# Moving the last token tile's products, its Gelu and four loads at the end of layer one's token loop

## The chip, the core and the metric

The kernel runs on one core of a Trainium2 chip. The metric is the device time of one launch in microseconds (us), the median of several runs. A core has five engines that run side by side and wait for each other by semaphores: TensorE (PE) multiplies matrices and writes the results to PSUM banks, VectorE (DVE) and ScalarE (ACT) do elementwise work and empty the banks, GpSimd (POOL) does elementwise work and issues some DMAs, and SyncE (SP) issues most DMAs. Each of them works through its own instructions strictly in the order in which the program issued them. So an instruction that waits holds up everything behind it on its engine.

## What is computed

Two layers, each a linear attention block and a gated block over 2048 tokens of width 512, all in float32. The change lies in the gated block of the first one:

```python
x = x + _A_ref(_layernorm(x), A_wqkv, A_wo)
x = x + _B_ref(_layernorm(x), B_w_in, B_w_sp, B_b_sp, B_w_out)     # and both once more: layer two

def _B_ref(x, w_in, w_sp, b_sp, w_out):
    z = _gelu(jnp.einsum("bsd,df->bsf", x, w_in))     # 512 -> 1792
    z1 = z[..., :896]
    z2 = _layernorm(z[..., 896:], axis=-1)
    g = jnp.einsum("ts,bsf->btf", w_sp, z2) + b_sp[None, :, None]
    return jnp.einsum("bsf,fd->bsd", z1 * g, w_out)
```

## The kernel before

Every float32 matrix product is made of three passes over operands that are split in two: a high part `h` (ScalarE copies the value into the rounded type, `high`, L220) and the rest `l` (VectorE subtracts, `low`, L223), and PE adds `h*h`, `h*l` and `l*h`. Big products are cut by a seven-product scheme (seven block products in place of eight), for which VectorE first forms sums and differences of blocks. They are called the fifth, sixth, seventh block and so on by the number of their product.

The program is unrolled; the order in which Python calls the helpers is the order on each engine. Three kinds of buffers matter here, each handed out by a first-in, first-out list: `pages` (22 tiles of 128x512), `quads` (6 tiles of 128x2048, which hold split weights and blocks) and `banks` (8 PSUM banks). A new owner of a buffer waits until the old owner's last reader is done. The sixth block's split takes the quad that held the high part of `xT[2]`, and P4's first raw weights the one that held its low part.

**The token loop.** `P2.run` takes the 16 token tiles of layer one (L = 0) through a pipeline of steps `s` = 1 to 18 (NT = 16). In a step, `c` finishes the attention of tile s-1, `d_high` and `d_low` transpose and split tile s-2 into `self.xT` (four tiles together make 512 tokens, so `xT[2]` are tiles 8 to 11 and `xT[3]` tiles 12 to 15), `e` multiplies tile s-3 with the second half of `w_in` into two banks, `e2` applies Gelu to them (L1076), `e3` takes the mean and variance (for tiles 14 and 15 on VectorE, `stats`, L365 and L367, with three small GpSimd instructions, L369 to L372), and `e4` normalises (L378). `first_a`, `first_b` and `first_out` (steps 15 to 17) begin the first half z1 for tokens 1024 to 2047. In steps 16 and 17 `e` and `e2` of tiles 13 and 14 stand near the head of the step; tile 15's stand after `tsplit(6)` and `e4(13)` in step 18.

**The blocks of `xT`.** z1 for the last 1024 tokens is made by the seven-product scheme: `raw(0)` and `raw(1)` (L1168) rebuild two blocks of `xT[2]` as h + l into the quad `self.B`; `T1` (L1202, L1203) turns the first into the fifth block, `T1split` splits it; `T2` makes two pairs of pages, `t2` (the sixth block, L1214 and L1216) and `b22` (the seventh, L1218 and L1219); `tsplit(6)` and `tsplit(7)` split these.

**The end.** `tail` then multiplies: `f(True)` for one piece of z1, three products with the fifth block `T[5]` into banks `v`, three with the sixth `T[6]`, three with the seventh `T[7]`, three with `xT[3]` itself, and three with `T[4]` (all `fmul`, L1161 to L1163, six matmuls each). Its results go through Gelu (`out`, L1151) and are stored to DRAM (L1153). The weights for `T[7]` come by six POOL DMAs (L211, `wfetch`) that are issued at the end of step 17.

**The spatial product.** `P4` follows: `w_sp` times z2, in steps `g`. Step g needs the raw weights (`fetch`, SP DMAs, L1743), their split (`sp`: `wsp`, L1764 on ScalarE and L1767 on VectorE) and the split part of z2 (`zahead`: L1872 and L1876, or L1852 to L1858 and then L220 and L223), then twelve matmuls (`mm`, L1989 to L1991). The raw weights live in halves of two quads, so the load of step g+4 waits until the split of step g has read its half. The four bias rows of `b_sp` are loaded by `loadb` (L2020, four SP DMAs into four pages): in layer one behind step g = 0 of P4, in layer two inside `tail`. They are first added at the end of P4's step 3.

Of the kernel before, what the change touches and what calls it, by code (L numbers as in the profile page):

```python
# [10 lines left out]
F32 = mybir.dt.float32  # L11
# [8 lines left out]
NT = S // P  # L20
# [138 lines left out]
def mixer_kernel(ctx: ExitStack, tc: tile.TileContext, x_in, wqkv, wo_d, win1_d, win2_d, wsp_d, bsp_d, wout_d,  # L159
# [671 lines left out]
    class P2:  # L831
# [378 lines left out]
        def T2(self):  # L1210
            h, l = (t.bitcast(F32) for t in self.xT[3])
            self.b22, self.t2 = ([pages.get(PAGE) for _ in range(2)] for _ in range(2))
            for c in range(2):
                nc.vector.tensor_add(self.b22[c], h[:, 2 + c], l[:, 2 + c])  # L1214
            for c in range(2):
                nc.vector.tensor_sub(self.t2[c], self.b22[c], self.B[:, 0, c])  # L1216
            for c in range(2):
                nc.vector.tensor_sub(self.b22[c], self.b22[c], h[:, c])  # L1218
                nc.vector.tensor_sub(self.b22[c], self.b22[c], l[:, c])  # L1219
# [11 lines left out]
        def tail(self):  # L1231
            V, A = nc.vector, nc.scalar.activation
            h, l = (t.bitcast(F32) for t in self.xT[3])
            L = self.L
# [48 lines left out]
            if L:  # L1283
# [2 lines left out]
                self.e4(NT - 4)  # L1286
                self.e4(NT - 3)
            quads.put(self.B)
            self.p4.fetch(3)
            ws = []  # L1290
            for f in range(3):
# [33 lines left out]
        def run(self, sums):  # L1325
# [4 lines left out]
            for s in range(1, NT + 3):  # L1330
# [42 lines left out]
                        self.d_high(s - 2)  # L1373
                        self.d_low(s - 2)
                if s == NT + 1:
                    self.raw(0)
                    self.T1()
                    self.T1split()
                    self.T2()
                    self.raw(1)  # L1380
                if s == NT + 2:
                    quads.put(*self.xT.pop(2))
                    self.tsplit(6)
                if s >= 4 and s != E4LATE:
                    self.e4(s - 4 - (s > E4LATE))
                self.qturn.load(s + 2)
                self.xturn.load(s - 1)
                if s >= 3:
                    if s not in (NT, NT + 1):
                        self.e(s - 3)  # L1390
                        self.e2(s - 3)
                    self.e3(s - 3)
                for _ in range(FONE.get(s, 0)):
                    self.f()
                if s in (15, 16, 17):
# [9 lines left out]
                    self.fsums.split(WADD[s - 1])  # L1405
                if s == NT:
                    self.B = quads.get([P, 2, 2, 512])
                    self.wf.extend(w1sums[f, 1] for f in range(3))
                self.fq.extend(self.fnext)
                self.fnext = []  # L1410
# [58 lines left out]
        def run2(self):  # L1469
            late = self.p1  # L1470
            for s in range(1, NT + 3):
# [5 lines left out]
                if s in self.qturn.by_pe:  # L1477
                    self.c(s - 1)
                    self.b_high(s)
                    self.c2(s - 1)  # L1480
                    late.late_phi_b()
                    self.b_low(s)
                    if s >= 2:
                        self.d_high(s - 2)
                        self.d_low(s - 2)
                    late.late()
                    self.c3(s - 1)
                    self.a2(s + 2)
                    late.late_phi_a()
                    self.a(s + 3)  # L1490
                else:
                    def b():
                        if s < NT:
                            self.b_high(s)

                    def bl():
                        if not pair:
                            self.a2_den(s + 2)
                        if s < NT:
                            self.b_low(s)  # L1500
                        if pair:
                            self.a2_den(s + 2)

                    if not pair:
                        if s >= FIRSTPAIR + 3:
                            self.a(s + 3)
                        b()
                        bl()
                    if s <= NT:
                        self.c(s - 1)  # L1510
                        self.c2(s - 1)
                    if s == NT:
                        quads.put(*self.W2)
                        pages.put(self.zbc)
                    ahead = s - 2 in self.xturn.by_pe

                    def turn():
                        self.d_high(s - 2)
                        self.d_low(s - 2)

                    def p():
                        self.a2_mul(s + 2)

                    def q():
                        if ahead:
                            turn()
                        if s <= NT:
                            self.c3(s - 1)
                        if pair or s < FIRSTPAIR + 3:
                            self.a(s + 3)  # L1530

                    def r():
                        if s <= NT + 1 and not ahead:
                            turn()

                    if pair:
                        def bp():
                            bl()
                            p()

                        def g():
                            if s - 6 >= FIRSTPAIR:
                                self.e4(s - 6)
                                self.e4(s - 5)

                        def ld():
                            self.wfetch()
                            self.wfetch()

                        if s == NT - 2:  # L1550
                            self.epair(s - 4, b, bp, q, r)
                        elif s == NT:
                            def q4():
                                q()
                                self.e4(NT - 8)
                                self.e4(NT - 7)

                            self.epair(s - 4, q4, ld, r)
                        elif s > NT:
                            def late4():  # L1560
                                self.T1split()
                                self.first_out(1, 2)
                                self.e4(NT - 6)
                                self.e4(NT - 5)

                            def late3():
                                self.raw(1)
                                quads.put(*self.xT.pop(2))
                                self.T2()
                                self.e3(NT - 4, False)  # L1570
                                self.e3(NT - 3, False)

                            self.epair(s - 4, late4, late3)
                        else:
                            self.epair(s - 4, b, bp, q, r, g)
                    elif s < FIRSTPAIR + 3:
                        p()
                        q()
                        r()
                    else:  # L1580
                        self.odd(s, p, q, r)
# [115 lines left out]
    class P4:  # L1697
# [622 lines left out]
        def run(self, nxt):  # L2320
            p2 = self.p2
            early = nxt is None
# [15 lines left out]
            for g in range(n):  # L2338
# [14 lines left out]
                    self.sums.tick()  # L2353
                if nxt is not None:
                    self.sums.halve(PARTS.get((p, k), -1), self.mark)
                if not early and g == 0:
                    self.loadb()
                if p in self.div:
                    if p == "P4" and k == 0 and "P5" in self.div:
                        for j in range(2):  # L2360
# [109 lines left out]
```

## Time and profile before

| | |
|---|---|
| median of 3 runs | 1349.79 us (1348.66 to 1350.32) |
| the profiled execution | 1349.34 us, of which 1347.6 us are the span of its instructions |
| PE | busy 1336.6 us, 99% of the span |
| DVE, ACT, POOL | busy 1074.6, 739.1 and 461.3 us |
| mean granted PE clock | 0.998 of full speed |
| layer one's token loop and tail | 129 to 352 us of the span: PE busy 218.4 of 223 us |
| layer one's P4 and after it | 352 to 683 us: PE busy 329.8 of 331 us |

A row of the timeline gives the start and the duration in us, the engine, the line, the operation, what it writes and reads, its shape, and how often it stands there in a row; in brackets stands how long the engine was idle before it and whom it waited for. Matmuls overlap: one of 128x512 lasts 0.39 us but the next starts 0.227 us after it. A row of the waits gives who waited for whom, the sum, how many times, and the longest.

### The profile page before, as it was taken

To read this page: it belongs to the slowest core of one execution; us is meant where nothing else is said; L and a number is where in the kernel's file an instruction comes from. 1 tells how busy PE (TensorE), PEld (TensorE's weight loads), DVE (VectorE), ACT (ScalarE), POOL (GpSimd) and SP (SyncE) were. 2 spreads that over 40 slices of the span, in tenths; PEclk is the share of its full clock that TensorE was granted. 3 is DMA by queue.
4 is the path that set the end of the run, shared out by engine and by line. 5 is a ranking of instruction groups with operands and counts; after the bars stand their busy time and mean duration, and the time that the engine had idled before them with its cause. 6 is when DMAs were issued, how large, how long until landed. Compare 5 with 4: busy or idle time off the path is not lost.

```text
span 1347.6 us, 19239 instructions
## 1 busy us (share of the span) xinstructions
PE 1336.6 (99%) x6533; PEld 1139.5 (85%) x6533; DVE 1074.6 (80%) x1687; ACT 739.1 (55%) x1250; POOL 461.3 (34%) x611
## 2 busy tenths in 40 slices
PE   9999999998999999999999999999999999999998
PEld 7888888887888888889988888888888888888898
DVE  7779877767799899898866778678689758899885
ACT  5764544445752256354666665557687433666454
POOL 3755775442026400301423444554531013122021
PEclk9999999999999999999999999999999999999999
DMA  5898599975879996794774562688777555579344
GB/s 183 292 307 271 169 299 293 302 225 196 266 252 377 332 295 191 271 319 94 178 159 129 132 154 73 193 240 262 236 220 234 167 161 174 176 243 319 123 76 66
DMA packets 172594, 291.34 MB, mean 216 GB/s; under 512 B 14544, under 2 KB 53456, under 8 KB 172240
## 3 DMA queue, kind: packets, MB, share of 16 engines
q1 hardware_dynamic: 153376, 250.92, 56.1%
q0 software_dynamic: 18976, 39.07, 13.6%
q8 instruction: 51, 0.84, 0.3%
q14 instruction: 47, 0.39, 0.1%
q10 hardware_dynamic: 144, 0.13, 0.0%
HBM read 205.39 MB, written 101.45 MB: 228 GB/s over the span
## 4 chain that ended last, share of the span: by engine, by line
PE 95%; DVE 2%; DMA 1%; ACT 1%; issue 0%; SPq 0%; POOL 0%; ACTq 0%; DVEq 0%
PE bank L234 13%; PE bank L236 13%; PE bank L235 13%; PE bank L1990 12%; PE bank L1991 12%; PE bank L1989 12%; PE bank L2187 3%; PE bank L2188 3%; PE bank L2189 3%; PE bank L1161 1%; PE bank L1163 1%; PE bank L1162 1%; PE bank L990 1%; PE bank L992 1%; PE bank L991 1%; PE bank L390 1%
## 5 line engine op out<-in xcount | busy, mean ns | idle before, releaser
L1989 PE MATMUL bank<-qd,pg 128*128 128x512 f32 x736 | 286.7, 390 | 0.7 <-ACT pg L1827 0.7
L1990 PE MATMUL bank<-qd,pg 128*128 128x512 f32 x736 | 286.6, 389 | 0.5 <-DVE qd L1767 0.5
L1991 PE MATMUL bank<-qd,pg 128*128 128x512 f32 x736 | 286.6, 389 | 0.0
L1764 ACT ACTIVATE qd<-qd 128x1024 fp32r<-128x1024 f32 x142 | 149.2, 1053 | 127.6 <-PE bank L1991 94.4
L1767 DVE TENSOR_TENSOR qd<-qd,qd 128x1024 fp32r<-128x1024 f32 x132 | 165.7, 1257 | 40.6 <-ACT qd L1764 40.4
L236 PE MATMUL bank<-qd,pg 128*128 128x512 f32 x448 | 174.8, 390 | 0.0
L1989 PEld LDWEIGHTS bank<-qd,pg 128*128 128x128 f32 x736 | 138.2, 188 | 30.0 <-ACT pg L1827 1.1
L1990 PEld LDWEIGHTS bank<-qd,pg 128*128 128x128 f32 x736 | 138.2, 188 | 29.5 <-DVE qd L1767 1.0
L1991 PEld LDWEIGHTS bank<-qd,pg 128*128 128x128 f32 x736 | 138.2, 188 | 28.9 <-DVE pg L1829 0.3
L2030 POOL TENSOR_TENSOR bg<-bg,pg 128x512 f32<-128x512 f32 x28 | 49.9, 1784 | 189.7 <-ACT qd L1764 92.9
L234 PE MATMUL bank<-qd,pg 128*128 128x512 f32 x264 | 103.3, 391 | 0.2 <-ACT pg L220 0.2
L235 PE MATMUL bank<-qd,pg 128*128 128x512 f32 x264 | 103.0, 390 | 0.0
L236 PEld LDWEIGHTS bank<-qd,pg 128*128 128x128 f32 x448 | 84.1, 188 | 18.1 <-DVE pg L223 0.4
L1673 POOL TENSOR_TENSOR pg<-pg,pg 128x512 f32<-128x512 f32 x48 | 70.0, 1458 | 71.8 <-DMA pg<-in_wsp_dram 64.5
L369 POOL TENSOR_SCALAR rs<-mv 128x1 f32<-128x1 f32 x76 | 23.8, 313 | 184.4 <-DVE mv L367 180.2
L2189 PE MATMUL bank<-wo,qd 128*128 128x256 f32 x288 | 81.5, 283 | 0.0
L2187 PE MATMUL bank<-wo,qd 128*128 128x256 f32 x276 | 78.2, 283 | 0.0
L2188 PE MATMUL bank<-wo,qd 128*128 128x256 f32 x276 | 78.1, 283 | 0.0
L220 ACT ACTIVATE pg<-pg 128x512 fp32r<-128x512 f32 (+1 forms) x86 | 49.9, 592 | 42.2 <-DVE pg L1858 20.0
L223 DVE TENSOR_TENSOR pg<-pg,pg 128x512 fp32r<-128x512 f32 (+1 forms) x84 | 54.7, 660 | 10.0 <-ACT pg L220 8.5
L549 POOL TENSOR_TENSOR pg<-pg,pg 128x512 f32<-128x512 f32 x30 | 39.9, 1331 | 59.8 <-DVE pg L543 58.0
L234 PE MATMUL bank<-bg,qd 128*128 128x448 f32 x160 | 59.0, 369 | 0.0
(297 smaller groups left out, 3361.8 us busy)
## 6 DMA issues: line engine op xcount, KB each, us to landing
qd<-s SPq DMA_DIRECT2D x62, 512.0 KB, 4.6
qd<-in_wsp_dram SPq DMA_DIRECT2D x40, 512.0 KB, 4.4
qd<-hP SPq DMA_DIRECT2D x40, 512.0 KB, 4.6
pg<-z SPq DMA_DIRECT2D x56, 256.0 KB, 5.3
pg<-in_wsp_dram SPq DMA_DIRECT2D x52, 256.0 KB, 4.5
s<-pg SPq DMA_DIRECT2D x48, 256.0 KB, 4.1
z<-pg SPq DMA_DIRECT2D x40, 256.0 KB, 3.6
pg<-w POOLq DMA_DIRECT2D x38, 256.0 KB, 4.9
```

What stands on the lines that cost most here:

```text
L234: nc.tensor.matmul(out, ah, bh, start=start, stop=False)
L235: nc.tensor.matmul(out, ah, bl, start=False, stop=False)
L236: nc.tensor.matmul(out, al, bh, start=False, stop=stop)
L1673: nc.gpsimd.tensor_tensor(t, a, b, op=OP.add)
L1764: self.mark = nc.scalar.activation(w[:, 0], r, AF.Copy)
L1767: nc.vector.tensor_sub(w[:, 1], r, w[:, 0].bitcast(F32))
L1989: m(out, h[:, o], w[:, 0, j, :], start=start, stop=False, skip_group_check=True)
L1990: m(out, h[:, o], w[:, 1, j, :], start=False, stop=False, skip_group_check=True)
L1991: m(out, l[:, o], w[:, 0, j, :], start=False, stop=stop, skip_group_check=True)
L2187: m(out, A, x, start=start and f == 0, stop=False, skip_group_check=True)
L2188: m(out, A, y, start=False, stop=False, skip_group_check=True)
L2189: m(out, B, x, start=False, stop=stop and f == 2, skip_group_check=True)
```

## The change

It touches the code of layer one's last three steps and of its tail; layer two keeps its order (`T3` is called there straight behind `T2`).

- `raw(0)` and `raw(1)` move from step 17 to the end of step 16, as soon as the quad `B` is taken.
- `T2` is cut in two: `T3` holds its last four instructions (the seventh block) and moves to step 18, behind `tsplit(6)`.
- In step 18 `e` and `e2` of tile 15 stand at the head, ahead of `tsplit(6)`, and `e3` of tile 14 moves there from step 17.
- `loadb` moves from P4's step 0 into `tail`, ahead of `fetch(3)`.

```diff
+        def T3(self):
+            h, l = (t.bitcast(F32) for t in self.xT[3])
             for c in range(2):
                 nc.vector.tensor_sub(self.b22[c], self.b22[c], h[:, c])
                 nc.vector.tensor_sub(self.b22[c], self.b22[c], l[:, c])
...
             quads.put(self.B)
+            if not L:
+                self.p4.loadb()
             self.p4.fetch(3)
...
                 if s == NT + 1:
-                    self.raw(0)
                     self.T1()
                     self.T1split()
                     self.T2()
-                    self.raw(1)
                 if s == NT + 2:
                     quads.put(*self.xT.pop(2))
+                    self.e(s - 3)
+                    self.e2(s - 3)
                     self.tsplit(6)
+                    self.T3()
+                    self.e3(s - 4)
                 if s >= 4 and s != E4LATE:
                     self.e4(s - 4 - (s > E4LATE))
                 self.qturn.load(s + 2)
                 self.xturn.load(s - 1)
                 if s >= 3:
-                    if s not in (NT, NT + 1):
+                    if s < NT:
                         self.e(s - 3)
                         self.e2(s - 3)
-                    self.e3(s - 3)
+                    if s != NT + 1:
+                        self.e3(s - 3)
...
                 if s == NT:
                     self.B = quads.get([P, 2, 2, 512])
+                    self.raw(0)
+                    self.raw(1)
...
-                if not early and g == 0:
-                    self.loadb()
```

Three places show how the order on the engines moves. The order of PE's instructions is the same before and after.

ScalarE, steps 17 and 18, before. The first row is the high part of the fifth block (`qd_19`), then `e4` of tile 12, a Gelu of `first_out`, the sixth block's high parts (`qd_20`), `e4` of tile 13, tile 15's two Gelus (`L1076`), and the seventh block's high parts (`bg_7`):

```order
L220 ACTIVATE qd_19_3633<-qd_18_3584 128x1024 [waits DVE_49]
L378 ACTIVATE z_z_3434<-z_z_3434,acc 128x896
L1151 ACTIVATE pg_348_3666<-bank_136_3586 128x512 [waits PE_49]
L220 ACTIVATE qd_20_3686<-pg_346_3638 128x512 [waits DVE_49]
L220 ACTIVATE qd_20_3686<-pg_347_3639 128x512
L378 ACTIVATE z_z_3536<-z_z_3536,acc 128x896 [waits Activation_49,Pool_49]
L1076 ACTIVATE z_z_3718<-bank_140_3692 128x448 [waits PE_49]
L1076 ACTIVATE z_z_3718<-bank_141_3705 128x448 [waits PE_49]
L220 ACTIVATE bg_7_3734<-pg_344_3636 128x512
L220 ACTIVATE bg_7_3734<-pg_345_3637 128x512
```
and after the change:

```order
L220 ACTIVATE qd_19_3634<-qd_18_3584 128x1024 [waits DVE_49]
L378 ACTIVATE z_z_3434<-z_z_3434,acc 128x896
L1151 ACTIVATE pg_348_3652<-bank_136_3588 128x512 [waits PE_49]
L1076 ACTIVATE z_z_3698<-bank_140_3672 128x448 [waits PE_49,Activation_49]
L1076 ACTIVATE z_z_3698<-bank_141_3685 128x448 [waits PE_49]
L220 ACTIVATE qd_20_3701<-pg_346_3639 128x512 [waits DVE_49]
L220 ACTIVATE qd_20_3701<-pg_347_3640 128x512 [waits DVE_49]
L378 ACTIVATE z_z_3536<-z_z_3536,acc 128x896 [waits Activation_49,Pool_49]
L220 ACTIVATE bg_7_3734<-pg_344_3637 128x512 [waits DVE_49]
L220 ACTIVATE bg_7_3734<-pg_345_3638 128x512 [waits DVE_49]
```
Tile 15's Gelus stand ahead of the sixth block's high parts and of `e4`, three rows earlier.

VectorE, step 17, before. The first row is the low part of tile 15's transpose, then `raw(0)`, `T1` and the low part of the fifth block (`qd_19`):

```order
L223 TENSOR_TENSOR qd_17_3273<-bank_139_3623,qd_16_3272 128x4x128 [waits Activation_49]
L1168 TENSOR_TENSOR qd_18_3584<-qd_14_2766,qd_15_2767 128x1024
L1202 TENSOR_TENSOR qd_18_3584<-qd_16_3272,qd_18_3584 128x1024 [waits DVE_49]
L1203 TENSOR_TENSOR qd_18_3584<-qd_18_3584,qd_17_3273 128x1024 [waits DVE_49]
L223 TENSOR_TENSOR qd_19_3633<-qd_18_3584,qd_19_3633 128x1024 [waits Activation_49]
```
and after (the row with x2 is both `raw`):

```order
L1168 TENSOR_TENSOR qd_18_3584<-qd_14_2766,qd_15_2767 128x1024 x2
L223 TENSOR_TENSOR qd_17_3273<-bank_139_3625,qd_16_3272 128x4x128 [waits Activation_49]
L1202 TENSOR_TENSOR qd_18_3584<-qd_16_3272,qd_18_3584 128x1024 [waits DVE_49]
L1203 TENSOR_TENSOR qd_18_3584<-qd_18_3584,qd_17_3273 128x1024 [waits DVE_49]
L223 TENSOR_TENSOR qd_19_3634<-qd_18_3584,qd_19_3634 128x1024 [waits Activation_49]
```
Both `raw` stand ahead of the row that waits for ScalarE, and `T1` follows that row at once.

SyncE, before: the last four stores of z1 (`L1153`), the bias rows, and the raw weights of P4's steps 6 and 7 (one row with x2) and 8:

```order
L1153 DMA z_0_3_2_3901<-pg_366_3899 128x512 [waits DMAHW6_49,Activation_49]
L1153 DMA z_0_2_3_3933<-pg_370_3931 128x512 [waits DMAHW7_49,Activation_49]
L1153 DMA z_0_2_4_3937<-pg_371_3935 128x512 [waits DMAHW0_49,Activation_49]
L1153 DMA z_0_2_5_3941<-pg_372_3939 128x512 [waits DMAHW1_49,Activation_49]
L2020 DMA pg_379_3975<-in_bsp_dram 128x512 [waits DMAHW5_49,DMAHW2_49]
L2020 DMA pg_380_3977<-in_bsp_dram 128x512 [waits DMAHW6_49,DMAHW3_49,PE_49]
L2020 DMA pg_381_3979<-in_bsp_dram 128x512 [waits DMAHW7_49,DMAHW4_49,PE_49]
L2020 DMA pg_382_3981<-in_bsp_dram 128x512 [waits DMAHW0_49,PE_49]
L1743 DMA qd_22_3817<-in_wsp_dram 128x2x512 [waits DVE_49] x2
L1743 DMA qd_21_3731<-hP_3_0_150 128x2x512 [waits DVE_49]
```
and after: z1's piece from `f(True)`, the bias rows, the raw weights of P4's steps 2 to 4 and the first two of nine stores of z1:

```order
L1146 DMA z_0_3_6_3784<-pg_358_3782 128x512 [waits DMAHW4_49,Activation_49]
L2031 DMA pg_359_3817<-in_bsp_dram 128x512 [waits DMAHW5_49,DMAHW0_49]
L2031 DMA pg_360_3819<-in_bsp_dram 128x512 [waits DMAHW6_49,DMAHW1_49]
L2031 DMA pg_361_3821<-in_bsp_dram 128x512 [waits DMAHW7_49,DVE_49]
L2031 DMA pg_362_3823<-in_bsp_dram 128x512 [waits DVE_49]
L1754 DMA qd_22_3825<-hP_1_0_148 128x2x512 [waits PE_49]
L1754 DMA qd_22_3825<-hP_1_1_152 128x2x512 [waits DMAHW2_49]
L1754 DMA qd_21_3731<-hP_2_0_149 128x2x512 [waits DMAHW3_49,DVE_49]
L1153 DMA z_0_3_3_3860<-pg_355_3736 128x512 [waits DMAHW4_49,Activation_49]
L1153 DMA z_0_3_4_3863<-pg_356_3737 128x512 [waits DMAHW5_49,Activation_49]
```
The bias rows now stand ahead of the raw weights of step 2; behind the last store of z1 the raw weights of step 6 follow directly.

Pages are handed out in turn, so taking four of them earlier gives other pages to the rows that follow. Among these are the split parts of z2 for P4's steps 3, 4 and 5 (the three `L220` rows on ScalarE with their `L223` on VectorE): before, one of the three high parts is written into a page that a store of z1 has yet to leave; after, all three are.

1 line of the change is left out of this document (added).

## The prediction

> **What bounds the kernel now.** I read the page's head first, then the waits of PE, then PE's timeline round the two waits that the change can touch, then what ScalarE, VectorE and SyncE did ahead of them.
>
> ```profile
> span 1347.6 us, 19239 instructions
> PE 1336.6 (99%) x6533; PEld 1139.5 (85%) x6533; DVE 1074.6 (80%) x1687; ACT 739.1 (55%) x1250; POOL 461.3 (34%) x611
> ```
>
> PE is busy for all but 11.0 us, so a change that leaves PE's work alone can win 11.0 us and what PE loses to a lower clock. The waits of PE from 250 to 480 us:
>
> ```profile
> PE bank L1161 <- ACT z_z L1076: 4.6, 1, 4.6
> PE bank L1989 <- ACT pg L1827: 0.7, 1, 0.7
> PE bank L1990 <- DVE qd L1767: 0.5, 1, 0.5
> ```
>
> The first is in the tail: the last product with the fifth block wants a bank that tile 15's Gelu (L1076) has not emptied. The third is in P4's step 6, where the split of raw weights is late. Here are both in PE's timeline, with a window that gives the granted clock (the 0.57) after the first:
>
> ```profile
> 325.40 0.39 PE L1161 MATMUL bank<-qd,pg 128*128 128x512 f32 x1
> ...
> 327.89 0.39 PE L1163 MATMUL bank<-qd,pg 128*128 128x512 f32 x1
> 332.83 0.80 PE L1161 MATMUL bank<-qd,pg 128*128 128x512 f32 x1 [4.55 <-ACT z_z L1076]
> ...
> 336.12 0.39 PE L1163 MATMUL bank<-qd,pg 128*128 128x512 f32 x1
> ...
> 351.99 0.39 PE L1989 MATMUL bank<-qd,pg 128*128 128x512 f32 x1
> ...
> 368.31 0.39 PE L1989 MATMUL bank<-qd,pg 128*128 128x512 f32 x1
> 369.24 0.50 PE L1990 MATMUL bank<-qd,pg 128*128 128x512 f32 x1 [0.55 <-DVE qd L1767]
> ...
> 370.51 0.39 PE L1989 MATMUL bank<-qd,pg 128*128 128x512 f32 x1
> ```
> ```profile
> 332.80:336.20 3.40, 3.37 (x9) 2.71 (x10) 3.28 (x7) 2.82 (x6) 3.30 (x7) 0.57 0.98 333
> ```
>
> From 351.99 to 368.31 PE starts 72 matmuls, one each 0.227 us. At that pace the matmul of 336.12, the ninth after the one of 327.89, would start at 329.94: the first wait costs 6.18 us. Of these 4.71 are the wait (332.83 less 327.89 less 0.227), and 1.47 are the low clock for the eight starts behind it. In the same way the third wait costs 0.83 (370.51 less 368.31 less six starts, 1.36).
>
> Why was the Gelu late? ScalarE had it behind the split of the sixth block and `e4`, and these behind VectorE:
>
> ```profile
> 321.63 1.06 ACT L220 ACTIVATE qd<-qd 128x1024 fp32r<-128x1024 f32 x1 [4.41 <-DVE qd L1203]
> 322.59 1.12 ACT L378 ACTIVATE z_z<-z_z,acc 128x896 f32<-128x896 f32 x1
> 323.62 0.58 ACT L1151 ACTIVATE pg<-bank 128x512 f32<-128x512 f32 x1
> 330.18 1.15 ACT L220 ACTIVATE qd<-pg 128x512 fp32r<-128x512 f32 x2 [5.99 <-DVE qd L1168]
> ...
> 332.26 0.95 ACT L1076 ACTIVATE z_z<-bank 128x448 f32<-128x448 f32 x2
> ```
> ```profile
> 313.31 1.43 DVE L223 TENSOR_TENSOR pg<-pg,pg 128x256 fp32r<-128x256 f32 x4
> 317.25 0.69 DVE L223 TENSOR_TENSOR qd<-bank,qd 128x512 fp32r<-128x512 f32 x1 [2.51 <-ACT qd L220]
> 317.86 1.22 DVE L1168 TENSOR_TENSOR qd<-qd,qd 128x1024 f32<-128x1024 f32 x1
> 319.11 1.22 DVE L1202 TENSOR_TENSOR qd<-qd,qd 128x1024 f32<-128x1024 f32 x1
> ...
> 325.07 1.29 DVE L1216 TENSOR_TENSOR pg<-pg,qd 128x512 f32<-128x512 f32 x2
> 326.27 0.69 DVE L1218 TENSOR_TENSOR pg<-pg,qd 128x512 f32<-128x512 f32 x1
> ...
> 328.93 1.22 DVE L1168 TENSOR_TENSOR qd<-qd,qd 128x1024 f32<-128x1024 f32 x1
> 330.07 1.14 DVE L365 BATCH_NORM_STATS2 st<-z_z 128x6 f32<-128x448 f32 x2
> ...
> 331.37 1.25 DVE L223 TENSOR_TENSOR qd<-pg,qd 128x512 fp32r<-128x512 f32 x2
> ```
>
> The sixth block was there at 326.36 (L1216), but its high part is written into a quad that `xT[2]` held (`qd_14`, now `qd_20`), and `raw(1)` reads that quad last: behind the last four instructions of `T2`, at 328.93. So ScalarE stood for 5.99 us until 330.18, and `e4` and the Gelus behind it. The Gelu needed nothing of this: between tile 15's matmuls and the one of 325.40 stand only the twelve of `f(True)`, so its banks had been filled by 322.9.
>
> **The change part by part.** The raw blocks are two instructions of 1.22. VectorE sat idle for 2.51 us ahead of 317.25, since 314.74; they end there at about 317.1, and cost nothing. If that idle time were gone they would push the chain back by 2.4. With `raw(0)` out of the way `T1` starts at 317.86 in place of 319.11, and all behind it moves by 1.25.
>
> *Gelu.* The high part of the fifth block starts at 320.38, `e4` at 321.34, `first_out` at 322.37, tile 15's Gelus at 322.9, and end by 323.9. PE wants the bank at 328.12 (327.89 and 0.227). Slack: over 4 us. The wait goes, and with it the low clock: 6.18 us.
>
> *Sixth block.* Ready at 326.36 less 1.25 = 325.1, its two splits on ScalarE and VectorE end by 326.4. Three products of 1.36 (six starts) from 325.40 end at 329.48, when PE needs it. Slack 3 us.
>
> *Seventh block.* `T3` runs behind that: 2.66 us (326.27 to 328.93) from 326.4, so until 329.0; then the statistics of tiles 14 and 15, 1.30 each (330.07 to 331.37), until 331.6; then its two low parts, 1.25, the first by 332.3. PE comes at 329.48 and 4.08 = 333.57, and needs the low part one start later. Slack 1.5 us, the smallest in the tail. Its weights come by POOL's six loads. Here are SP's stores of the last of them, their time to landing, and the times to landing of the six loads:
>
> ```profile
> 324.59 2.02 SPq L753 DMA_DIRECT2D w1s<-pg  x4
> ...
> w1s<-pg SPq DMA_DIRECT2D x4, 256.0 KB, 2.6
> ...
> DMA to landing us min/median/max: 3.0/4.4/6.2
> ```
>
> They stood behind the GpSimd instructions of tile 14's statistics; with `e3` moved these follow them. What is left ahead of the last two loads are these stores, which SP issues behind `first_out`, so by 1.25 earlier, until 325.4, and which land 2.6 later; the two loads issue by 328.5 and land by 334.7 even with the longest 6.2, and the third product needs them at 336.3. Tile 14's mean and deviation reach `e4` later than the loads, but ScalarE comes to that `e4` only at about 335, and GpSimd has its input by 330.4.
>
> *The rest of the tail* is products whose blocks were early enough before and come earlier still. P4 then starts at 351.99 less 6.18 = 345.81. Step 0's raw weights waited for `raw(1)` and come earlier. VectorE, after the seventh block: two subtractions to 334.1, three sums of 0.66 and the low part of `T[4]` to 337.3, three sums behind PE's seventh products to 339.1, a part of z2 (0.75) and step 0's low part (1.23) to 341.1. Slack 4.7.
>
> *Bias rows.* They stood between the stores of z1 and the raw weights of steps 6 and 7. The rows are from SP's timeline, the chain of waits (a transfer from its issue to its landing) and ScalarE's waits:
>
> ```profile
> 355.92 3.31 SPq L2020 DMA_DIRECT2D pg<-in_bsp_dram  x4
> ...
> 359.28 7.51 DMA qd<-in_wsp_dram
> ...
> ACT qd L1764 <- DMA qd<-in_wsp_dram: 3.6, 1, 3.6
> ACT pg L220 <- DMA z<-pg: 3.8, 1, 3.8
> ```
>
> Step 6's load was issued 7.3 us after P4 began, and ScalarE stood 3.6 us for it. Now SP reaches it right behind the last store, at about 347.1 (the last products end at 346.0, the last two Gelus at 0.55 each and the store's issue of 0.48 follow, some of it side by side), 1.3 us after P4 begins. The raw weights of step 2 wait for the bias rows instead: two of these go into pages that VectorE reads last at 334.1, so step 2's load goes at 334.7, over 9 us before ScalarE takes it at 344.2; even the 7.51 that step 6's load took would do. The 0.83 us of step 6 are thus gone too, if nothing takes their place.
>
> *Pages.* Something could. The split parts of z2 for steps 3 to 5 now go into pages that stores of z1 read. In before one such wait held ScalarE for 3.8 us (the last row above). The nine stores:
>
> ```profile
> L1153 SPq DMA_DIRECT2D z<-pg x9: 389/477/1220, 347.0 to 353.8; - x9
> ...
> DMA to landing us min/median/max: 4.4/4.9/5.4
> ```
>
> ScalarE ends the Gelus of the `xT[3]` products at 343.6 (PE's end of 341.9 and three of 0.55), then makes a part (0.6) and step 2's split (1.05), and the next Gelu, of `T[4]`'s first product, by 345.6. Its store frees the page of step 4's high part: issued at 345.65, landed 4.9 later, at 350.5. ScalarE then needs 0.6 for that part and 1.05 for the split of step 3's weights, VectorE 1.23 more: ready at 353.4. PE needs it at 345.81 and three steps of 2.72 and one start: 354.2. Slack 0.8; for steps 4, 5, 6 and 7 I get 1.2, 2.1, 1.1 and 1.4. So I take this new wait at nothing, between a gain of nothing and a loss of 1.5 us (the longest landing of such a store anywhere in the trace, below, is 7.2: 2.3 more than 4.9, less 0.8).
>
> ```profile
> DMA to landing us min/median/max: 2.0/4.8/7.2
> ```
>
> *Sum:* 6.18 + 0.83 = 7.0 us. Everything behind P4's start is PE's own work with 0.7 us of waits up to 480 us, and moves as a whole.
>
> [...]
>
> **The rivals.**
> *A new wait at P4's start.* The pages hold ScalarE so that steps 3 to 6 come late. For it: the slack of 0.8 is smaller than the spread of landings. Against it: 5.4 is the longest of these nine. Price 0.8 to 3: 1343.6 to 1345.8.
> *The seventh block becomes late.* Slack 1.5, and VectorE is busy without a gap from 317 on. It would give back 1 to 3: 1343.8 to 1345.8.
> *A collision of VectorE and GpSimd moves.* PE's 0.7 wait at 472 us goes back to one VectorE row, beside gate products on GpSimd:
>
> ```profile
> 461.95 4.54 DVE L1829 TENSOR_TENSOR pg<-pg,pg 128x384 fp32r<-128x384 f32 x1
> ...
> 472.27 0.55 DVE L1829 TENSOR_TENSOR pg<-pg,pg 128x384 fp32r<-128x384 f32 x1
> ```
>
> The same instruction takes 0.55 elsewhere. Should a shift of loads against splits put it on another row, or on two, the price runs from -0.7 to +4.0: 1342.1 to 1346.8. [...]
> *No change.* The 4.55 would be put down to the wrong producer. Against it: the waiting matmul waits for ScalarE alone, and started between the ends of the two Gelus (0.95 for both from 332.26). Price nothing: 1349.8.
> *Slower.* The stores' pages, as in the first rival, but so late that ScalarE and VectorE, with every later split queued behind, hold PE for longer than both waits did: it decides from a landing of 4.9 + 0.8 + 7.0 = 12.7 us; 15.4 would give 1352.5. No store came near it.
>
> **How the numbers follow.** The profiled execution took 1349.34, 0.45 under the median of the three; its sum is 1342.3, and on the median 1349.79 - 7.0 = 1342.8. Chances: both waits go 0.58, new wait at P4's start 0.21, seventh block late 0.06, collision 0.06, no change 0.06, slower 0.03. The range goes down by the 0.7 of the collision's good end and 0.6 for the spread of a median, to 1341.5, and up to 1345.8 for the first two rivals; what is left out is some 0.15. About 0.2% (2.7 us) is what a measurement of this kernel can tell: faster 0.90, same 0.07, slower 0.03.
>
> **What would show it.** Right: no wait of PE for L1076, a granted clock of 1 throughout the tail, P4's first matmul at about 345.8, no wait of ScalarE for step 6's raw weights. Wrong: a wait of PE in P4's steps 3 to 7 behind a ScalarE wait for a store of z1, or a wait of the seventh product for VectorE.

## The result and the profile after

| | before | after |
|---|---|---|
| median of 6 runs each, us | 1350.05 (1348.66 to 1351.97) | 1342.40 (1341.37 to 1345.24) |
| time after / before, 95% interval | | 0.9946 (0.9933 to 0.9959) |
| profiled execution, us | 1349.34 | 1341.83 |
| its span, us | 1347.6 | 1340.1 |
| mean granted clock of TensorE | 0.998 | 1.000 |

By the medians the change made the kernel 7.65 us faster, to 1342.4 where 1342.8 was predicted; between the two profiled executions it is 7.5 us, against the 7.0 of the prediction's sum. What follows accounts for these 7.5. The busy times on the page after the change:

```profile
PE 1334.2 (100%) x6533; PEld 1138.6 (85%) x6533; DVE 1074.3 (80%) x1687; ACT 739.8 (55%) x1250; POOL 464.1 (35%) x611
```

PE's waits from 250 to 480 us were three, and are one, a new one:

```profile
PE bank L2001 <- DVE qd L1778: 0.6, 1, 0.6
```

PE's timeline has the first product with the fifth block, P4's first matmul, and the new wait in P4's step 3. Behind it is the row of the window in which the granted clock (third number from the end) was 0.57 before:

```profile
325.48 0.39 PE L1161 MATMUL bank<-qd,pg 128*128 128x512 f32 x1
...
345.88 0.39 PE L2000 MATMUL bank<-qd,pg 128*128 128x512 f32 x1
...
354.04 0.39 PE L2000 MATMUL bank<-qd,pg 128*128 128x512 f32 x1
354.99 0.50 PE L2001 MATMUL bank<-qd,pg 128*128 128x512 f32 x1 [0.56 <-DVE qd L1778]
```
```profile
332.80:336.20 3.40, 3.40 (x17) 2.81 (x16) 3.40 (x7) 2.62 (x4) 1.47 (x2) 1.00 0.70 264
```

From the first product to P4 it is 345.88 - 325.48 = 20.40 us, where it was 351.99 - 325.40 = 26.59: 6.19 us less. I use this stretch as the measure for every run below, since it leaves out the few tenths by which executions differ ahead of the tail. ScalarE's and VectorE's rows show what brought it about and what is late next:

```profile
322.91 0.97 ACT L1076 ACTIVATE z_z<-bank 128x448 f32<-128x448 f32 x2
324.60 1.24 ACT L220 ACTIVATE qd<-pg 128x512 fp32r<-128x512 f32 x2 [0.72 <-DVE pg L1216]
...
350.15 0.63 ACT L220 ACTIVATE pg<-pg 128x512 fp32r<-128x512 f32 x1 [3.48 <-DMA z<-pg]
352.09 0.63 ACT L220 ACTIVATE pg<-pg 128x512 fp32r<-128x512 f32 x1 [1.31 <-DMA z<-pg]
```
```profile
325.27 1.29 DVE L223 TENSOR_TENSOR qd<-pg,qd 128x512 fp32r<-128x512 f32 x2
...
331.77 1.27 DVE L223 TENSOR_TENSOR bg<-pg,bg 128x512 fp32r<-128x512 f32 x2
...
353.71 1.23 DVE L1778 TENSOR_TENSOR qd<-qd,qd 128x1024 fp32r<-128x1024 f32 x1 [0.26 <-ACT qd L1775]
```

The sixth block's high part is written at 324.60 behind its sum (L1216), where it stood 5.99 us for `raw(1)`. In P4 ScalarE stands 3.48 and 1.31 us for stores of z1 whose pages it is to write, step 3's split ends at 353.71 + 1.23 = 354.94, and PE, which wanted it at 354.27, loses 0.84 us (the steps of 0.95 and 0.34 us behind 354.04, less two of 0.227). The nine stores:

```profile
L1153 SPq DMA_DIRECT2D z<-pg x9: 382/423/1088, 341.3 to 348.4; - x9
...
DMA to landing us min/median/max: 4.4/5.4/6.1
```

PE's wait at 472 us, which went back to a collision of VectorE and GpSimd, is gone. Here are two rows of PE before, then rows of VectorE after:

```profile
471.21 0.39 PE L1991 MATMUL bank<-qd,pg 128*128 128x512 f32 x1
472.28 0.50 PE L1989 MATMUL bank<-qd,pg 128*128 128x512 f32 x1 [0.69 <-ACT pg L1827]
```
```profile
453.91 2.16 DVE L1829 TENSOR_TENSOR z_z<-z_z,z_z 128x384 f32<-128x384 f32 x1
456.00 2.13 DVE L1830 TENSOR_TENSOR z_z<-z_z,z_z 128x128 f32<-128x128 f32 x1
458.06 0.55 DVE L1840 TENSOR_TENSOR pg<-pg,pg 128x384 fp32r<-128x384 f32 x1
```

The collision itself has not gone. The row that took 4.54 us beside GpSimd's products now takes 0.55 (the last row above). But two rows ahead of it take 2.16 and 2.13 us beside the same products, where the same instructions take 0.55 and 0.28 at 463.7 and 464.2. What changed is the time: the last of VectorE's long rows ended 114.5 us after P4's start (466.49 less 351.99) and now ends 112.3 after it (458.13 less 345.88), and PE no longer waits. In PE's timeline before, the wait and the slow starts round it between 466.9 and 473.5 us cost 1.27 us over the pace of 0.227; after, there is no such gap. The terms are then 6.19 in the tail, 0.83 in step 6 and 1.27 at the collision, less 0.84 in step 3: 7.45 of the 7.5 us.

### The profile page after: what moved, and what is told of

Same layout as the page of the kernel before. It is cut to its first block, busy times and chain, and to the rows that moved or that the text cites. A ratio compares the mean times of both kernels' runs of the same rounds, so it can differ in the third digit from the quotient of the medians.

```text
span 1340.1 us, 19243 instructions
## 1 busy us (share of the span) xinstructions
PE 1334.2 (100%) x6533; PEld 1138.6 (85%) x6533; DVE 1074.3 (80%) x1687; ACT 739.8 (55%) x1250; POOL 464.1 (35%) x611
## 4 chain that ended last, share of the span: by engine, by line
PE 95%; DMA 2%; DVE 2%; ACT 1%; issue 0%; POOL 0%; SPq 0%; DVEq 0%; ACTq 0%
PE bank L234 13%; PE bank L236 13%; PE bank L235 13%; PE bank L2001 12%; PE bank L2000 12%; PE bank L2002 12%; PE bank L2198 3%; PE bank L2199 3%; PE bank L2200 3%; PE bank L990 1%; PE bank L991 1%; PE bank L992 1%; PE bank L1163 1%; PE bank L1162 1%; PE bank L1161 1%; PE bank L390 1%
## 5 line engine op out<-in xcount | busy, mean ns | idle before, releaser
L1778 DVE TENSOR_TENSOR qd<-qd,qd 128x1024 fp32r<-128x1024 f32 x132 | 168.6, 1279 | 37.6 <-ACT qd L1775 37.4
L220 ACT ACTIVATE pg<-pg 128x512 fp32r<-128x512 f32 (+1 forms) x86 | 50.0, 592 | 45.8 <-DVE pg L1869 19.9
L223 DVE TENSOR_TENSOR pg<-pg,pg 128x512 fp32r<-128x512 f32 (+1 forms) x84 | 54.5, 657 | 11.3 <-ACT pg L220 10.6
```

The lines of the kernel that those rows point to most:

```text
L1778: nc.vector.tensor_sub(w[:, 1], r, w[:, 0].bitcast(F32))
```

## The experiments

All twelve kernels compute the whole result. "To P4" is the stretch from the first product with the fifth block to P4's first matmul in the profiled execution, "rest" the one from there to the end of the span. Ratios are to the kernel before on the same chip.

| kernel | to P4 | rest | ratio, 95% interval |
|---|---|---|---|
| before | 26.59 | 995.6 | |
| changed | 20.40 | 994.2 | 0.9946 (0.9933 to 0.9959) |
| raw blocks alone | 26.58 | 993.6 | 0.9993 (0.9983 to 1.0003) |
| Gelu alone | 30.64 | 993.5 | 1.0016 (1.0007 to 1.0024) |
| raw blocks and statistics | 20.40 | 994.3 | 0.9953 (0.9941 to 0.9966) |
| bias rows alone | 26.83 | 993.9 | 0.9996 (0.9988 to 1.0005) |
| changed, again | 20.40 | 994.4 | 0.9958 (0.9945 to 0.9971) |
| changed, bias rows back | 20.40 | 995.4 | 0.9959 (0.9946 to 0.9972) |
| changed, bias rows in the second step | 20.40 | 995.2 | 0.9954 (0.9942 to 0.9966) |
| changed, statistics back | 20.83 | 994.0 | 0.9961 (0.9949 to 0.9973) |
| changed, 1 more subtraction | 20.40 | 996.3 | 0.9954 (0.9939 to 0.9969) |
| changed, 2 more | 21.60 | 997.0 | 0.9973 (0.9961 to 0.9985) |
| changed, 3 more | 22.81 | 1000.0 | 0.9977 (0.9967 to 0.9988) |
| changed, 4 more | 26.90 | 996.4 | 0.9985 (0.9974 to 0.9996) |

**Raw blocks alone.** My theory was that the quad held the sixth block, and through it the Gelu; the rival that the Gelu's place in the order alone made it late.

```diff
                 if s == NT + 1:
-                    self.raw(0)
                     self.T1()
                     self.T1split()
                     self.T2()
-                    self.raw(1)
...
                     self.B = quads.get([P, 2, 2, 512])
+                    self.raw(0)
+                    self.raw(1)
```

> The kernel before, with the two raw blocks moved to the end of step 16 and nothing else. Theory (the quad of xT[2], read last by raw(1), held the sixth block's split and through it the Gelu): ScalarE makes the sixth block's high part by about 326, tile 15's Gelu follows by 328.2 against 328.12 when PE wants its bank, so the first wait (4.6 us) and the low clock behind it go. But POOL's loads of the seventh block's weights still stand behind tile 14's statistics, which VectorE makes by about 329.1: the loads issue at 330.6 to 334.1 and land 4.4 later, against 333.57 to 336.3, so the seventh block's products wait 2 to 3 us. Step 6's wait of 0.8 stays. Gain 3 to 4.5 us: 1345.5 to 1347. Rival (the Gelu's place in the order is what made it late, the quad is incidental): the wait for L1076 stays above 3 us, gain under 1 us.

ScalarE's Gelu and PE's timeline, then POOL's six loads for the seventh block (first and last start; then issue to landing), and two windows with the granted clock. In this trace the windows of 1 us that lie wholly inside the slow stretch, from 337 to 342 us, read 0.50, and those ahead of it (330 to 336) and behind it (343 to 352) read 1.00. So I take the clock as half or whole, and a mean of 0.78 over 1.00 us as half for 0.44 of it:

```profile
326.95 0.95 ACT L1076 ACTIVATE z_z<-bank 128x448 f32<-128x448 f32 x2
```
```profile
333.68 0.39 PE L1163 MATMUL bank<-qd,pg 128*128 128x512 f32 x1
336.20 0.77 PE L1161 MATMUL bank<-bg,pg 128*128 128x512 f32 x1 [2.14 <-DMA pg<-w1s]
336.77 0.63 PE L1162 MATMUL bank<-bg,pg 128*128 128x512 f32 x1
338.09 0.80 PE L1163 MATMUL bank<-bg,pg 128*128 128x512 f32 x1 [0.70 <-DMA pg<-w1s]
...
342.53 0.56 PE L1161 MATMUL bank<-bg,pg 128*128 128x512 f32 x1
```
```profile
L211 POOL DMA_DIRECT2D pg<-w1s x6: 557/571/782, 331.2 to 334.1; - x6
...
DMA to landing us min/median/max: 4.9/6.5/6.8
```
```profile
335.50:336.50 1.00, 0.29 (x1) 0.33 (x2) 1.00 (x2) 1.00 (x2) 0.41 (x2) 0.78 1.09 401
...
342.00:343.00 1.00, 1.00 (x4) 0.74 (x4) 0.23 (x1) 0.00 (x0) 0.00 (x0) 0.56 0.00 0
```

The quad was the cause: with nothing else moved the Gelu ends at 327.9, its wait is gone, and the sixth block comes in time. And the whole gain is taken by what is late next, the loads behind tile 14's statistics, as expected in kind. The two waits are 2.84 us, inside the 2 to 3 that I had. But I had a gain of 3 to 4.5 left and there was none: the clock was halved from 336.06 to 342.88, and the stretch is as long as before to 0.01 us.

**Gelu alone.**

```diff
                     quads.put(*self.xT.pop(2))
+                    self.e(s - 3)
+                    self.e2(s - 3)
                     self.tsplit(6)
...
-                    if s not in (NT, NT + 1):
+                    if s < NT:
```

> The kernel before, with tile 15's products and Gelu at the head of step 18 and nothing else. Theory (the quad): PE's wait for the Gelu goes (Gelu by about 324.2), but the sixth block's high part still stands behind raw(1) until 330.2, so PE waits there instead: high part at 330.8, low part at 331.4 to 332 against 329.48, 1.5 to 2.5 us, and the loads for the seventh block, still behind tile 14's statistics, cost 2 to 3 us more. [...] Gain 1 to 3 us: 1347 to 1349. Rival (Gelu order alone decides): the whole 6.2 us are gained, 1343.6.

```profile
330.81 0.39 PE L1163 MATMUL bank<-qd,pg 128*128 128x512 f32 x1
332.42 0.49 PE L1161 MATMUL bank<-qd,pg 128*128 128x512 f32 x1 [1.22 <-ACT qd L220]
333.62 0.80 PE L1162 MATMUL bank<-qd,pg 128*128 128x512 f32 x1 [0.71 <-DVE qd L223]
...
341.32 0.47 PE L1161 MATMUL bank<-bg,pg 128*128 128x512 f32 x1 [0.61 <-DMA pg<-w1s]
...
343.15 0.50 PE L1163 MATMUL bank<-bg,pg 128*128 128x512 f32 x1 [1.13 <-DMA pg<-w1s]
```

The wait for the Gelu is gone, and PE waits for the sixth block's split instead (1.22 and 0.71), then for the loads. The places were right, and the sign was wrong: 4.05 us longer to P4 in this execution, and 0.16% by the runs, since the clock fell twice (0.5 lasted from 333.56 to 336.96, and from 343.80 to 350.62):

```profile
333.30:333.80 0.50, 0.18 (x1) 0.18 (x2) 0.50 (x2) 0.50 (x1) 0.42 (x2) 0.76 0.88 184
336.50:337.50 1.00, 1.00 (x5) 0.82 (x4) 1.00 (x3) 0.87 (x2) 1.00 (x3) 0.77 1.01 248
343.50:344.00 0.50, 0.50 (x3) 0.43 (x2) 0.00 (x0) 0.50 (x2) 0.00 (x0) 0.80 1.15 385
350.50:351.00 0.50, 0.50 (x3) 0.42 (x2) 0.50 (x2) 0.50 (x2) 0.00 (x0) 0.88 0.00 0
```

The rival, 1343.6, is out.

**Raw blocks and statistics.** The first edit, and tile 14's statistics behind the sixth block's split:

```diff
                     self.tsplit(6)
+                    self.e3(s - 4)
...
-                    self.e3(s - 3)
+                    if s != NT + 1:
+                        self.e3(s - 3)
```

> The kernel before, with the raw blocks moved and tile 14's statistics on GpSimd one step later; Gelu order, the rest of T2 and the bias rows as before. Theory: all of the 6.2 us of the first wait goes, but for up to 0.4 that the Gelu and the sixth block's low part may be late (they are reckoned at 328.2 against 328.12 and at 330.35 against 330.4); step 6's 0.8 stays or turns into a smaller wait. 1343 to 1344. Rival (the earlier Gelu is needed): a wait for L1076 of 1 us or more is left, over 1344.5.

```profile
326.67 0.39 PE L1161 MATMUL bank<-qd,pg 128*128 128x512 f32 x1
...
347.07 0.39 PE L1991 MATMUL bank<-qd,pg 128*128 128x512 f32 x1
```
```profile
327.96 0.95 ACT L1076 ACTIVATE z_z<-bank 128x448 f32<-128x448 f32 x2
```

These two edits hold the whole gain of the tail. The Gelu, in its old place, ends at 328.9, 0.5 us ahead of 326.67 + 2.72 = 329.39, when PE wants the bank. Neither its new place nor `T3` is needed for the time.

**Changed, statistics back.** `e3(NT - 2)` in step 17 again, everything else as changed.

```diff
                     self.T3()
-                    self.e3(s - 4)
...
-                    if s != NT + 1:
-                        self.e3(s - 3)
+                    self.e3(s - 3)
```

> The changed kernel with tile 14's statistics back in step 17 on GpSimd, all else as changed. Theory: POOL's six loads for the seventh block then stand behind statistics whose input VectorE has ready at about 326 to 331 in the new order, so the last of them issue 1 to 4 us later; a wait of the seventh block's products for their weights, 0 to 2 us: the same to 2 us slower than the changed kernel. Rival (the loads wait for the stores of the weight sums anyway, so the move is idle): no difference, and the loads issue at the same times.

```profile
L211 POOL DMA_DIRECT2D pg<-w1s x6: 557/571/782, 329.3 to 332.1; - x6
```

Counted from the first product with the fifth block, the last load goes 2.7 us earlier than with the raw blocks alone, since `T3` no longer stands ahead of the statistics, and 2.3 later than in the changed kernel, where it goes at 328.9; PE loses 0.43 us. So `T3` in step 18 and `e3` in step 18 are two ways to the same end; `e3` is the better by a little, and the run times don't tell the two apart.

**Bias rows: alone, taken back, and one step late.**

```diff
             quads.put(self.B)
+            if not L:
+                self.p4.loadb()
             self.p4.fetch(3)
...
-                if not early and g == 0:
-                    self.loadb()
```

The second kernel takes this out of the changed one. The third has it one step of P4 later, so that raw weights of step 6 are issued ahead of the bias rows:

```diff
             quads.put(self.B)
-            if not L:
-                self.p4.loadb()
...
+                if not early and g == 1:
+                    self.loadb()
```

> The kernel before, with the bias rows' load moved into the tail and nothing else. Theory (SP stood on the bias rows ahead of step 6's raw weights): the first wait stays as it was (4.6 and the low clock), the wait in P4's step 6 (0.55, costing 0.8) goes, and a wait in step 3 for the split of its weights appears, 0.3 to 0.6 us, since the pages of the split parts of z2 now follow stores of z1. Net 0.2 to 0.5 us: 1349.2 to 1350. Rival (the pages were no matter, the step 3 wait in the changed kernel comes from the shifted tail): no wait in step 3, gain 0.8.

> The changed kernel itself, on the chip of the three that follow, as their measure. Theory: 7.0 to 8 us below the kernel before, with a wait of about 0.5 us in P4's step 3 for VectorE's split (L1778). Rival (that wait is a chance of one execution): no wait there this time.

> The changed kernel with the bias rows back in P4's first step, all else as changed. Theory (pages): the wait in P4's step 3 (0.56) goes, since the split parts of z2 for steps 3 and 4 go into other pages than those that stores of z1 read, and ScalarE no longer waits for stores there; the wait in step 6 for its raw weights (0.5 to 0.8 us) is back. Net between -0.5 and +0.5 us against the changed kernel. Rival (the step 3 wait comes from the seventh block's tail of work on VectorE and ScalarE): the step 3 wait stays and step 6's is added, +0.5 to +0.8.

> The changed kernel with the bias rows in P4's second step instead of the tail: SP issues step 6's raw weights ahead of them. Theory: neither step 3's wait nor step 6's: the pages of steps 3 and 4 are free long before, and step 6's raw weights are issued right behind the last store. 0.5 to 0.9 us below the changed kernel. Rival (each order only moves the wait): a wait of 0.3 us or more in steps 3 to 7, and no gain over the changed kernel.

Alone, the edit took step 6's wait away. It brought none in step 3, where I had expected one: on that the rival was right. The changed kernel showed its step 3 wait a second time (0.39 listed, 0.66 lost). With the bias rows back, step 3 lost 0.35 us, and step 6 cost 0.53 and not 0.83; with the raw blocks and statistics alone, where the rows were never moved, step 6 cost nothing. ScalarE's rows for step 6's raw weights in these two, bias rows back and raw blocks and statistics:

```profile
361.46 1.06 ACT L1773 ACTIVATE qd<-qd 128x1024 fp32r<-128x1024 f32 x1 [2.75 <-DMA qd<-in_wsp_dram]
```
```profile
359.94 1.06 ACT L1766 ACTIVATE qd<-qd 128x1024 fp32r<-128x1024 f32 x1 [1.05 <-DMA qd<-in_wsp_dram]
```

Over all profiles the picture is plainer. In the five with the rows in P4's first step ScalarE stood for step 6's raw weights, for 3.59 (before), 2.75, 2.05 (Gelu alone), 1.33 (raw blocks alone) and 1.05 us; in the eight with the rows in the tail it never did. PE paid for the two longest of these waits alone, 0.83 and 0.53 us. So the bias rows' place is worth between nothing and 0.83 us of one execution, and the runs see no difference.

With the rows in the second step, step 3's wait was gone and step 6 cost 0.37, for another reason: VectorE, which adds the rows at the end of step 3, stood 2.62 us for one of them to land, with step 6's low part behind that addition. PE waited again at the collision (0.69), and the order gained nothing that can be measured on the changed kernel, as its rival said.

The collision cost PE between 0.9 and 1.3 us in four of the six profiles that have the rows in P4 and next to nothing (up to 0.1) in the other two. Of the eight that have them in the tail it cost 1.7 and 2.9 in two (three and four subtractions, below), and up to 0.2 in the others. That is a count, not a cause.

**One to four subtractions more.** To size the seventh block's slack and the price of one wait by itself, VectorE gets n more subtractions behind `T3` (n = 1 to 4), into a part of `B` that nothing reads any more.

```diff
                     self.T3()
+                    self.idle(n)
...
+        def idle(self, n):
+            h = self.xT[3][0].bitcast(F32)[:, 0:2]
+            for _ in range(n):
+                nc.vector.tensor_sub(self.B[:, 0], h, self.B[:, 0])
```

> The changed kernel with one more VectorE subtraction (128x1024, 1.22 us, into a block that nothing reads any more) behind T3, ahead of the statistics. It makes the seventh block's low part 1.22 us later. Measured from the first product with the fifth block to P4's first matmul, the changed kernel takes 20.40 us. Theory (slack of 1.5 us there): the low part ends at about 333.6 against 333.8, no wait, 20.4 to 20.5, no change in time. Rival (the slack was reckoned too wide): a wait of the seventh product for VectorE, 0.3 to 1.2 us.

> The same with two subtractions, 2.44 us. Theory: one wait of the seventh product for VectorE, 2.44 less the slack of 1.4: 1.0 us. A wait of this size costs itself alone (PE waited 1.0 us elsewhere without a lower clock): 21.4 us to P4. Rival (any wait in the tail lowers the clock): a granted clock below 1 behind it, 22.5 us or more.

> The same with three subtractions, 3.66 us. One wait of about 2.2 us. [...]

> The same with four subtractions, 4.88 us. One wait of about 3.4 us, shorter than the 4.7 of the kernel before. [...]

The seventh product's wait with two and with three, each with two waits in P4 behind it, and with four; then windows of the granted clock with three and with four:

```profile
336.11 0.50 PE L1162 MATMUL bank<-bg,pg 128*128 128x512 f32 x1 [0.86 <-DVE bg L223]
...
357.35 0.50 PE L2006 MATMUL bank<-qd,pg 128*128 128x512 f32 x1 [0.72 <-ACT qd L1781]
358.61 0.50 PE L2007 MATMUL bank<-qd,pg 128*128 128x512 f32 x1 [0.76 <-DVE qd L1784]
```
```profile
337.04 0.50 PE L1162 MATMUL bank<-bg,pg 128*128 128x512 f32 x1 [2.11 <-DVE bg L223]
...
358.21 0.51 PE L2006 MATMUL bank<-qd,pg 128*128 128x512 f32 x1 [0.69 <-ACT qd L1781]
360.42 0.79 PE L2007 MATMUL bank<-qd,pg 128*128 128x512 f32 x1 [1.71 <-DVE qd L1784]
```
```profile
338.11 0.80 PE L1162 MATMUL bank<-bg,pg 128*128 128x512 f32 x1 [3.38 <-DVE bg L223]
```
```profile
337.00:342.00 5.00, 4.96 (x22) 4.11 (x23) 5.00 (x8) 3.17 (x4) 1.74 (x3) 1.00 0.45 114
...
360.00:360.40 0.40, 0.00 (x0) 0.00 (x0) 0.40 (x2) 0.40 (x2) 0.00 (x0) 0.63 0.07 20
363.00:364.00 1.00, 1.00 (x4) 0.76 (x4) 1.00 (x3) 1.00 (x4) 0.00 (x0) 0.74 0.61 234
```
```profile
337.00:337.50 0.50, 0.00 (x0) 0.00 (x0) 0.40 (x3) 0.00 (x0) 0.37 (x2) 0.83 0.17 66
344.00:344.50 0.50, 0.50 (x4) 0.40 (x3) 0.00 (x0) 0.50 (x2) 0.00 (x0) 0.84 0.94 344
```

To P4 it took 0, 1.20, 2.41 and 6.50 us more. VectorE's work behind them starts 2.40 us later with two and 3.66 with three (1.22 to 1.26 each), so the slack is 1.20 to 1.25 us, where I had reckoned 1.5. The first three doses cost what PE waits, to 0.2 us (idle for 1.02 and 2.27 us round the waits of 0.86 and 2.11). The fourth adds 3 us of halved clock, from 337.33 to 344.16. With three the wait of 2.11 in the tail left the clock at 1.00 (337 to 342 above), but in the same run the clock fell at the waits of 0.69 and 1.71 in P4, and was half from 360.10 to 363.52. With two it fell behind the waits of 0.72 and 0.76: the windows below, which put the half clock from 359.72 to 363.12. With one, where PE waited 0.64 until 355.11 and 0.76 until 356.37, it stayed at 1.00 from 355 to 360. Here are two and one:

```profile
358.00:360.00 2.00, 1.39 (x5) 1.12 (x6) 1.15 (x2) 2.00 (x5) 0.00 (x0) 0.93 0.02 5
360.00:364.00 4.00, 4.00 (x12) 3.16 (x11) 3.95 (x7) 3.35 (x8) 0.00 (x0) 0.61 0.67 238
```
```profile
355.00:357.00 2.00, 1.14 (x4) 0.73 (x5) 1.91 (x2) 1.39 (x4) 0.00 (x0) 1.00 0.08 28
357.00:360.00 3.00, 2.86 (x13) 2.05 (x12) 1.75 (x4) 3.00 (x6) 0.00 (x0) 1.00 0.54 175
```

The free subtraction was free in the tail alone. In P4 one subtraction cost 2.36 us in step 3, where the changed kernel lost 0.84: the store of `T[4]`'s first product, which holds a page of step 4, went out 1.18 us after P4 began and not 0.22. With two and three, waits in step 3 and the clock that fell behind them make up most of the larger rests in the table. The runs are less sharp: with one subtraction their ratio cannot be told from the changed kernel's.

## Why the prediction was right, and where not

*The first wait.* Right in cause and size. The Gelu started at 322.91 (predicted 322.9), the sixth block was split by 326.56 (326.4), the seventh block's first low part ended at about 332.4 (332.3), P4 began at 345.88 (345.81), and 6.19 us went where 6.18 were predicted. The raw blocks alone show the quad as the cause, and the Gelu alone, where PE went on waiting for the sixth block, shows the same from the other side.

*The seventh block's loads.* The prediction counted the move of tile 14's statistics as something that keeps its slack. It is more: without it and `T3` the loads take back all of the 6.2 us.

*What the Gelu's move does.* The prediction let the Gelu's new place carry the step ("Slack: over 4 us"). That is true of the changed kernel, but the Gelu would have been in time in its old place too, by 0.5 us. By itself the move makes the kernel slower.

*Pages.* This is the term that was mis-sized: the new wait was taken "at nothing" on a slack of 0.8. It cost 0.84 us. The path was as written: step 4's high part waited for the store of `T[4]`'s first product, and step 3's split stood behind it. This store is

```profile
346.10 1.09 SPq L1153 DMA_DIRECT2D z<-pg  x1
```

It went out at 346.10 where the text had 345.65, and took 5.89 us to land and not 4.9, so that its page came free 1.44 us later than reckoned, against a slack of 0.8. The first rival, a new wait at P4's start, thus came at the bottom of its 0.8 to 3, and the likeliest case as written (no new wait) did not quite. A wait of PE in P4's step 3 behind a store of z1 is also what the text had named as a sign of being wrong; it was there, and was small. With the bias rows alone moved there was none, so the pages matter together with the earlier tail.

*The collision.* Priced as a rival, from -0.7 to +4.0. It moved to other rows of VectorE, as the rival said it might, and gave 1.27, since more than the one listed wait of 0.69 hung on it. This is what put the total past 7.0, and the prediction had no step that says which way it goes. That the total came within 0.5 us is thus in part luck: 0.84 lost to the pages and 1.27 won at the collision, neither in the sum, largely cancel.

*Bias rows.* The 0.83 of step 6 went, and for the reason given: step 6's load was issued 3.2 us after P4 began (349.09) and not 7.3, later than the 1.3 of the text but early enough, and ScalarE never stood for it with the rows in the tail. But 0.83 is the price of one execution. With the rows in P4's first step and the tail mended ScalarE stood 1.05 and 2.75 us for that load, and PE lost nothing and 0.53.

*The seventh block.* The slack of 1.5 was 1.2 to 1.25 by the subtractions. It was the smallest in the tail, and it held.

*Waits and the clock.* My expectations for the raw blocks alone and the Gelu alone priced waits of 1.5 to 3 us at a full clock. That was an estimate of mine that no run had shown, and it failed: the clock was half for 6.82 us in the first, and for 3.40 and 6.82 in the second. No term of the prediction's sum rested on it.

## What to carry to other kernels

When an engine waits for a producer that is early enough by its own inputs, look at the buffer that the instruction ahead of it on that engine is to write, and who reads that buffer last: here one addition on VectorE, moved one step, freed a quad, a split and a Gelu. Before counting on such a gain, mend the next thing on the path with it: the raw blocks without the loads were worth nothing, the Gelu without the raw blocks less than nothing. A buffer that a store has yet to leave is as much a wait as a late operand (ScalarE stood 3.48 us for one here), and a slack smaller than the spread of landings (0.8 here, against 4.4 to 6.1 us for nine stores) should be given a price.

## What the runs showed of the hardware

The granted clock of TensorE did not go by the length of one wait alone. One of 2.11 us left it at 1.00 (three subtractions), one of 2.14 halved it (raw blocks alone); waits of 0.64 and 0.76 left it at 1.00 (one subtraction), and behind 0.72 and 0.76 it fell (two). In the kernel before it fell inside the wait of 4.55, as these windows of 0.50 us show (half for 0.16 and 0.26 of them):

```profile
332.00:332.50 0.50, 0.00 (x0) 0.00 (x0) 0.50 (x2) 0.50 (x2) 0.42 (x2) 0.84 0.61 184
335.50:336.00 0.50, 0.50 (x3) 0.40 (x2) 0.50 (x2) 0.20 (x1) 0.50 (x2) 0.74 1.19 361
```

Every stretch of half clock whose two ends I read in this way, with PE's waits at or just ahead of its start:

| run | waits, us (the last until) | half clock from, to | lasted, us |
|---|---|---|---|
| before | 4.55 (332.83) | 332.34, 335.76 | 3.42 |
| raw blocks alone | 2.14 (336.20) | 336.06, 342.88 | 6.82 |
| Gelu alone | 1.22, 0.71 (333.62) | 333.56, 336.96 | 3.40 |
| Gelu alone | 0.61, 1.13 (343.15) | 343.80, 350.62 | 6.82 |
| two subtractions | 0.72, 0.76 (358.61) | 359.72, 363.12 | 3.40 |
| three subtractions | 0.69, 1.71 (360.42) | 360.10, 363.52 | 3.42 |
| four subtractions | 3.38 (338.11) | 337.33, 344.16 | 6.83 |

In two of the longer ones PE waited again while the clock was half: 0.70 with the raw blocks alone (until 338.09), 0.39 and 0.17 with the Gelu alone (until 345.09 and 346.45). What decides whether the clock falls, and for how long, these runs do not show. What they show is the price: the waits of 2.84 us with the raw blocks alone cost 6.18 us to P4 (26.58 less 20.40), the wait of 2.11 with three subtractions cost 2.41 (22.81 less 20.40).
